# Column sums over the token blocks on GpSimd, and a new order of all steps, in an attention and feed-forward kernel

## The chip, the cores and the metric

The kernel runs on one core of one Trainium2 chip. The metric is the device time of one execution in microseconds (us); the median of the runs counts. The core has five engines with a queue of its own each: TensorE (PE, matrix products, with its weight loads shown as PEld), VectorE (DVE), ScalarE (ACT), GpSimd (POOL), and SyncE (SP), which issues DMAs. An engine works off its queue in order and waits on semaphores for what other engines make. Sums of products are built up in PSUM, which has eight banks.

## What is computed

There are B = 8 batches, H = 8 heads, S = 512 tokens, Ns = 32 state rows and D = 64 channels. Tokens attend to the state rows, state rows attend to the tokens, and both results pass through one feed-forward layer with 512 inputs, 2048 hidden units and 512 outputs.

```python
scores = scale * np.matmul(x, state.transpose(0, 1, 3, 2))
a = np.exp(scores - scores.max(-1, keepdims=True))
a /= a.sum(-1, keepdims=True) + 1e-09
xread = np.matmul(a, state)
scores2 = scale * np.matmul(state, x.transpose(0, 1, 3, 2))
a2 = np.exp(scores2 - scores2.max(-1, keepdims=True))
a2 /= a2.sum(-1, keepdims=True) + 1e-09
sread = np.matmul(a2, x)
attn = np.concatenate([xread, sread], axis=2)
# x: attn with the heads side by side, 8 * 544 rows of 512
h = x @ w_in
s = np.sin(alpha * h)
out = (h + s * s / (alpha + 1e-09)) @ w_out
```

The second softmax uses the same exponentials as the first, summed over the 512 tokens instead of over the 32 state rows: these are the column sums of the title.

## The kernel before, in words

The kernel has no loops over tiles in its code. A class has one short method for each step, and a long string, ORDER, names every step with its arguments in the order in which it is to be issued. Each engine gets its share of the steps in that order. Arguments name the batch or tile, the piece, the PSUM bank and, at the end, the engine (A is ACT, V is DVE, G is POOL). A tile is the 512 tokens of a batch (tiles 0 to 7) or all 256 state rows (tile 8). Heads are held in two groups g of four; a batch's tokens in four blocks i of 128.

For each batch:

- `lx` loads x with a DMA on POOL's queue; `pk` copies it in another arrangement (xp); `td` transposes it with a DMA on SP's queue (xT). For batches 0 and 1 PE transposes instead (`xtq`, `xt`, copies `xq` and `xc`).
- `sc` (PE) makes the scores; `ex` (ACT) the exponentials E, with tokens on the partitions; `rs` and `rr` (DVE) the sums over the state rows and their reciprocals; `nm` (POOL before) multiplies them in, giving A; `ad` (a DMA on SP) transposes A to AT. For batch 0, `at` and `ac` do so with PE and a copy.
- `m` (PE) multiplies the state with a quarter of w_in, M, in products that use a 64 by 32 part of PE's array each, eight side by side; `me` (ACT or DVE) copies M from PSUM to SBUF.
- `w` (PE) multiplies E, summed over the tokens, with x: the unnormalised result of the state rows, 16 products. `cs` (PE) multiplies each of the four token blocks of E with a column of ones, once for either row r of a pair of heads, into 64 of the 128 PSUM partitions: the column sums, 8 products of half width for a batch. `rc` (DVE) takes the reciprocal of them and `xs` (DVE) multiplies it in, into xs_all.

For each tile t and each of 16 blocks f of 128 hidden units:

- `h` (PE) makes the hidden values in two products (four for tile 8, which reads xs_all of all batches and w_in); for tile 0 the two are separate steps, `hg`.
- `si` (ACT) takes the sine, `sq` (ACT, DVE or POOL) squares it, `gt` (DVE) multiplies by 1/alpha and adds h, giving gT, the input of the second product. gT lies in a pool of 38 buffers.
- `o` (PE) adds up the output of 128 rows (st) over the 16 blocks f, in one PSUM bank; `oc` (ACT or DVE) copies it to one of six buffers and `os` stores it with a DMA on SP's queue. The last part of tile 7 is split into two pieces of columns (`oh`, `och`, `osh`).

A step may use a PSUM bank only after the bank's last value has been read. Two steps of one tile's output need not be neighbours: `o` has two arguments f0 and f1, and ORDER names the run f0 to f1 of blocks each time, always from 0 upward. `warm_up` steps issue products of zeros, whose results nobody reads.

Lines of the profile that the prediction uses: 201 products of elementwise type (squares, and A), 255 the cast of the first state rows, 282 the loads of w_in, 399 `sc`, 410 `rs`, 416 `rr`, 406 `ex`, 450 `w`, 461 `cs`, 468 `rc`, 471 `xs`, 488 `m`, 496 `me`, 537, 543 and 552 `h`, 560 `si`, 569 `sq` on ACT, 576 `gt`, 587 `o`, 595 `oc`, 602 and 605 `os` (605 for the state rows).

Of the kernel before, what the change touches and what calls it, by code (L numbers as in the profile page):

```python
# [21 lines left out]
touch_x l_s01 consts touch lq.0.S ident_ l_alpha lq.1.S zero.0 warm_up.7.512.3 exp_table lq.2.S  # L22
zero.1 identf.V lq.3.S s01_c.G l_st li.0 xq.0.A s01_t.4 li.1 xtq.0.5 warm_up.1.384.3 xq.1.A
s01_k.1.V s01_k.0.A li.2 xtq.1.6 warm_up.2.448.3 xc.0.0.0.V xq.2.A xc.0.0.1.V lo.0 al_t.7 xq.3.A
xtq.2.0 warm_up.1.384.3 al_c inva sc.0.0.1 lo.1 xc.0.1.0.A warm_up.1.256.3 xtq.3.2 warm_up.2.128.3
ex.0.0 warm_up.2.128.4 lx.1.0.1 warm_up.2.128.5 xc.0.1.1.V warm_up.2.128.6 warm_up.2.128.7 rs.0.0
sc.0.1.0 li.3 st_t.0.3 ex.0.1 rr.0.0 st_t.1.4 lo.2 st_c.0.0.V st_c.0.1.A warm_up.2.128.5
warm_up.2.128.6 warm_up.2.128.1 st_c.1.0.A rs.0.1 warm_up.2.128.2 warm_up.2.128.7 nm.0.0.0.4.G
warm_up.2.128.0 warm_up.2.128.5 st_c.1.1.A warm_up.2.128.3 warm_up.2.128.6 warm_up.2.128.1 rr.0.1
warm_up.2.128.2 sin_table warm_up.2.128.7 warm_up.2.128.0 nm.0.1.0.4.G at.0.0.5 warm_up.2.128.3  # L30
ac.0.0.V m.0.0.6.4 m.1.0.1.2 lo.3 at.0.1.7 me.0.0.0.V me.0.0.1.A warm_up.2.128.0 warm_up.2.128.3
me.1.0.1.A ac.0.1.V hg.0.2.0.5 me.1.0.0.V hg.0.1.0.4 hg.0.2.1 hg.0.1.1 hg.0.0.0.0 lx.2.0.1 si.0.2
hg.0.0.1 m.1.1.6.3 si.0.1 m.0.1.7.2 hg.0.3.0.1 me.0.1.1.A sq.0.2.V hg.0.3.1 sq.0.1.G me.1.1.0.V
me.1.1.1.A warm_up.2.128.2 gt.0.2 si.0.0 warm_up.2.128.2 warm_up.2.128.6 warm_up.2.128.3
warm_up.2.128.2 warm_up.2.128.6 me.0.1.0.A gt.0.1 sq.0.0.G m.0.2.3.2 si.0.3 m.1.2.5.6 hg.0.4.0.7
me.0.2.0.V me.0.2.1.A hg.0.4.1 sq.0.3.G hg.0.6.0.4 me.1.2.1.V hg.0.6.1 si.0.4 hg.0.7.0.3 hg.0.11.0.2
me.1.2.0.V si.0.6 hg.0.7.1 sq.0.4.G hg.0.5.0.6 gt.0.0 hg.0.5.1 si.0.7 hg.0.11.1 hg.0.8.0.5 hg.0.8.1
sq.0.6.A gt.0.3 sq.0.7.G o.0.3.0.2.0 si.0.5 gt.0.4 o.0.3.2.3 o.0.0.0.2.1 si.0.11 o.0.0.2.3 gt.0.6
sq.0.5.G o.0.0.3.4 o.0.2.0.1.7 si.0.8 o.0.3.3.5 sq.0.11.A gt.0.7 hg.0.9.0.4 sq.0.8.G o.0.2.1.2
gt.0.5 o.0.2.2.4 hg.0.9.1 gt.0.11 o.0.0.4.5 hg.0.10.0.3 si.0.9 o.0.2.4.5 gt.0.8 o.0.0.5.6 o.0.3.5.6  # L40
sq.0.9.A o.0.3.6.8 pk.1.0.V hg.0.10.1 xt.1.1.6 pk.1.1.V si.0.10 gt.0.9 xt.1.0.2 xc.1.1.0.A sq.0.10.G
o.0.2.5.6 xc.1.1.1.V xc.1.0.0.A o.0.0.6.7 xc.1.0.1.V o.0.0.7.8 o.0.2.6.7 sc.1.1.5 gt.0.10 sc.1.0.4
m.0.3.6.2 ex.1.0 o.0.2.7.8 me.0.3.0.V o.0.1.0.3.3 me.0.3.1.V o.0.1.3.6 hg.0.13.0.6 o.0.1.6.7 ex.1.1
rs.1.0 hg.0.13.1 m.1.3.2.4 si.0.13 o.0.1.7.8 rr.1.0 rs.1.1 nm.1.0.0.4.G o.0.1.8.9 hg.0.12.0.5
o.0.3.8.9 rr.1.1 hg.0.12.1 me.1.3.0.V o.0.0.8.9 nm.1.1.0.4.G o.0.1.9.10 o.0.0.9.10 me.1.3.1.V
si.0.12 o.0.0.10.11 o.0.3.9.11 sq.0.13.G ad.1 hg.0.15.0.2 sq.0.12.A o.0.1.10.12 hg.0.15.1 gt.0.12
o.0.2.8.10 si.0.15 o.0.2.10.11 gt.0.13 o.0.0.11.12 hg.0.14.0.4 sq.0.15.A hg.0.14.1 o.0.3.11.13
si.0.14 gt.0.15 o.0.0.12.13 o.0.1.12.13 o.0.3.13.14 sq.0.14.A pk.2.0.V o.0.1.13.14 pk.2.1.V h.1.2.5
gt.0.14 h.1.4.6 td.2 si.1.2 lx.3.0.1 h.1.0.2 si.1.4 o.0.0.13.15 sq.1.2.V h.1.1.4 si.1.0 gt.1.2
sq.1.4.G o.0.3.14.16 si.1.1 o.0.2.11.13 sq.1.0.A oc.0.3.V h.1.6.5 sq.1.1.G gt.1.4 o.0.2.13.14 os.0.3  # L50
h.1.3.0 si.1.6 gt.1.0 o.0.1.14.16 si.1.3 sq.1.6.G h.1.13.6 gt.1.1 oc.0.1.A o.0.2.14.15 o.0.0.15.16
si.1.13 h.1.15.2 sq.1.3.G lx.4.0.1 gt.1.6 os.0.1 o.0.2.15.16 oc.0.0.A h.1.5.4 sq.1.13.V oc.0.2.V
si.1.15 h.1.7.3 os.0.0 gt.1.3 o.1.1.0.1.5 si.1.5 os.0.2 h.1.8.1 sq.1.15.G gt.1.13 o.1.1.1.2 si.1.7
o.1.2.0.2.7 sq.1.5.A o.1.1.2.3 sq.1.7.G h.1.12.0 gt.1.15 si.1.8 h.1.9.6 gt.1.5 o.1.2.2.3 si.1.12
sq.1.8.G o.1.2.3.5 gt.1.7 si.1.9 o.1.1.3.4 h.1.10.2 sq.1.12.A pk.3.1.V h.1.11.4 sq.1.9.G gt.1.8
o.1.2.5.6 si.1.10 o.1.2.6.7 gt.1.12 h.1.14.3 si.1.11 sq.1.10.G o.1.2.7.8 gt.1.9 sc.2.1.1 si.1.14
o.1.1.4.7 sq.1.11.A pk.3.0.V sq.1.14.G o.1.1.7.8 gt.1.10 td.3 o.1.2.8.9 sc.2.0.0 o.1.1.8.9 gt.1.11
o.1.1.9.10 ex.2.0 o.1.3.0.2.6 gt.1.14 o.1.3.2.4 o.1.2.9.10 o.1.3.4.5 o.1.2.10.12 ex.2.1 o.1.2.12.13
rs.2.0 o.1.1.10.11 m.2.2.2.4.3.0 rr.2.0 rs.2.1 o.1.2.13.14 nm.2.0.0.4.G me.2.3.0.A o.1.2.14.15 w.0.1
rr.2.1 me.2.2.1.A me.2.3.1.V o.1.3.5.6 nm.2.1.0.4.G me.2.2.0.A o.1.3.6.7 o.1.2.15.16 cs.0 oc.1.2.A  # L60
m.2.0.3.4.0.2 ad.2 rc.0 o.1.3.7.8 me.2.1.1.A o.1.3.8.9 sc.3.0.7 xs.0.1 me.2.1.0.A o.1.1.11.12 os.1.2
me.2.0.0.V sc.3.1.2 me.2.0.1.A o.1.1.12.13 o.1.3.9.10 xs.0.0 pk.4.1.V pk.4.0.V td.4 o.1.3.10.11
ex.3.0 o.1.1.13.16 ex.3.1 rs.3.0 o.1.3.11.13 oc.1.1.A o.1.3.13.14 rr.3.0 h.2.0.0 rs.3.1 nm.3.0.0.4.G
os.1.1 o.1.3.14.16 si.2.0 rr.3.1 h.2.1.3 oc.1.3.V nm.3.1.0.4.G h.2.2.4 h.2.8.1 os.1.3 h.2.3.7 ad.3
si.2.2 o.1.0.0.3.2 si.2.8 sq.2.0.V o.1.0.3.4 sq.2.2.G gt.2.0 h.2.4.5 si.2.1 o.1.0.4.6 si.2.3
sq.2.8.G o.1.0.6.7 gt.2.2 h.2.9.6 si.2.4 o.2.3.0.1.0 o.1.0.7.8 sq.2.1.G o.1.0.8.9 sq.2.3.A gt.2.8
o.1.0.9.10 h.2.5.4 si.2.9 gt.2.3 o.1.0.10.11 sq.2.4.G o.1.0.11.12 si.2.5 h.2.7.1 gt.2.1 o.1.0.12.13
sq.2.9.A sq.2.5.G o.1.0.13.14 gt.2.4 o.1.0.14.15 si.2.7 o.1.0.15.16 o.2.0.0.1.7 gt.2.9 o.2.0.1.2
oc.1.0.A h.2.6.3 sq.2.7.G gt.2.5 o.2.3.1.2 os.1.0 o.2.3.2.3 si.2.6 h.2.10.5 o.2.3.3.4 sq.2.6.A
o.2.3.4.5 gt.2.7 h.2.11.6 si.2.10 h.2.12.2 gt.2.6 si.2.11 o.2.0.2.3 sq.2.10.G o.2.0.3.4 o.2.3.5.6  # L70
si.2.12 h.2.15.4 h.2.13.1 sq.2.11.A gt.2.10 sq.2.12.G o.2.0.4.5 si.2.15 h.2.14.3 gt.2.11 o.2.3.6.7
si.2.13 o.2.0.5.6 sq.2.15.G gt.2.12 o.2.0.6.8 si.2.14 o.2.3.7.9 sq.2.13.A o.2.3.9.10 gt.2.15
sq.2.14.G o.2.0.8.11 gt.2.13 o.2.0.11.12 sc.4.0.5 sc.4.1.6 gt.2.14 o.2.3.10.12 ex.4.0 o.2.3.12.13
w.1.2 cs.1 o.2.0.12.13 rc.1 o.2.3.13.15 ex.4.1 o.2.3.15.16 m.3.0.4.1.3.5 rs.4.0 oc.2.3.A o.2.0.13.14
me.3.1.0.A o.2.0.14.15 os.2.3 me.3.0.0.V o.2.1.0.1.6 me.3.0.1.A o.2.1.1.2 o.2.0.15.16 rr.4.0 rs.4.1
o.2.1.2.3 me.3.1.1.A nm.4.0.0.4.G h.3.1.0 oc.2.0.A o.2.1.3.4 rr.4.1 xs.1.0 m.3.2.3.4.1.5 si.3.1
nm.4.1.0.4.G os.2.0 xs.1.1 h.3.0.7 me.3.2.0.V h.3.2.2 ad.4 me.3.3.0.V o.2.1.4.6 lx.5.0.1 o.2.2.0.1.3
me.3.3.1.V si.3.2 o.2.2.1.3 si.3.0 h.3.6.1 sq.3.1.V sq.3.2.G me.3.2.1.V h.3.14.5 si.3.6 o.2.2.3.4
gt.3.1 o.2.2.4.5 sq.3.0.G si.3.14 o.2.2.5.7 gt.3.2 o.2.2.7.8 sq.3.6.A o.2.2.8.9 h.3.8.4 sq.3.14.G
gt.3.0 h.3.5.0 si.3.8 gt.3.6 h.3.15.2 si.3.5 o.2.2.9.10 sq.3.8.G gt.3.14 o.2.2.10.11 h.3.9.7 si.3.15  # L80
h.3.7.1 si.3.9 sq.3.5.G gt.3.8 o.2.2.11.13 si.3.7 h.3.10.5 sq.3.9.G o.2.2.13.14 sq.3.15.A gt.3.5
# [76 lines left out]
class Steps:  # L158
# [449 lines left out]
    def oh(k, t, st, half, bank):  # L608
        k.o(t, st, 0, k.FT, bank, half=half)
# [54 lines left out]
```

## Time and profile before

| | |
|---|---|
| median of 3 runs | 221.41 us (221.36 to 221.83) |
| the profiled execution | 221.22 us |
| its span, from first to last event | 219.2 us |
| TensorE busy | 211.4 us |
| column sums on PE (line 461) | 64 products |
| warm-up products (line 303) | 66 |

The profile is of one execution. A page of it gives for each engine the time in which it was busy, a chain of work followed back from the last instruction, and groups of instructions with their number, busy time, mean length, and the idle time before them with what ended it. A timeline lists instructions by start time. A matmul's length includes the time in which its result runs out of the array while the next one is already under way, so the distance from start to start tells what one costs in a stream; a few records of matmuls are missing.

### The profile page before, as it was taken

How to read it: one execution, taken by the hardware profiler on the slowest of the kernel's cores; microseconds unless marked ns; L12 is line 12 of the kernel's file. 1: busy time of each engine (PE TensorE's matmuls, PEld its weight loads, DVE VectorE, ACT ScalarE, POOL GpSimd, SP SyncE). 2: the span in 40 equal slices, each digit the busy share in tenths (PEclk: the TensorE clock that was granted, in tenths of full speed). 3: DMA queues.
4: the chain of work that ended last, by engine and by line, in shares of the span. 5: the costliest groups of instructions: out<-in, count | busy, mean ns of one | idle time of the engine just before them, and what ended most of it. 6: DMA issues, size and time to landing. Idle time of an engine off the chain costs nothing.

```text
span 219.2 us, 4303 instructions
## 1 busy us (share of the span) xinstructions
PE 211.4 (96%) x1593; PEld 104.5 (48%) x1619; DVE 162.9 (74%) x287; ACT 173.4 (79%) x297; POOL 106.2 (48%) x114
## 2 busy tenths in 40 slices
PE   7989999999999999999999999999999999999994
PEld 3744544444444534444454444454445555665452
DVE  3769996999787789989888788888667987661201
ACT  4799778997998979898996999798848896785111
POOL 5959533895195647753943387273501082121000
PEclk9999999999999999999999999999999999999999
DMA  6999999987491029167145327470220211012042
GB/s 195 178 206 204 205 204 146 217 169 133 101 238 48 3 92 143 57 144 96 48 79 131 109 71 96 134 110 0 48 100 0 98 48 48 0 51 96 1 143 96
DMA packets 38052, 23.48 MB, mean 107 GB/s; under 512 B 20992, under 2 KB 33680, under 8 KB 38032
## 3 DMA queue, kind: packets, MB, share of 16 engines
q1 hardware_dynamic: 26128, 15.08, 26.5%
q0 software_dynamic: 11648, 8.13, 26.0%
q8 instruction: 12, 0.20, 0.3%
q14 instruction: 8, 0.07, 0.1%
q10 hardware_dynamic: 256, 0.01, 0.1%
HBM read 17.44 MB, written 8.91 MB: 120 GB/s over the span
## 4 chain that ended last, share of the span: by engine, by line
PE 90%; DMA 6%; POOL 1%; issue 1%; ACT 0%
PE o_ps L587 54%; PE h_ps L537 22%; DMA w_in_sb<-in_moe_w_in_dram 5%; PE m_ps L488 4%; PE h_ps L543 3%; PE h_ps L552 2%; PE w_ps L450 2%; PE s_ps L399 2%; PE w_ps L461 1%; DMA s<-in_state_dram 1%; POOL w_in_sb L282 1%; PE x_ps L376 0%; POOL st_nat L267 0%; POOL s01b L255 0%; ACT o_sb L595 0%
## 5 line engine op out<-in xcount | busy, mean ns | idle before, releaser
L587 PE MATMUL o_ps<-w_out_sb,gT 128*128 128x512 bf16 (+2 forms) x542 | 133.9, 373 | 1.6 <-issue 1.0
L576 DVE SCALAR_TENSOR_TENSOR gT<-s,inva_sb,h_ps 128x512 bf16<-128x512 bf16 (+1 forms) x144 | 96.8, 713 | 20.4 <-POOL s L201 10.8
L201 POOL TENSOR_TENSOR s<-s 128x512 bf16<-128x512 bf16 (+1 forms) x75 | 75.9, 1022 | 64.4 <-ACT s L560 62.7
L560 ACT ACTIVATE s<-h_ps,alpha_sb 128x512 bf16<-128x512 f32 (+1 forms) x144 | 88.8, 670 | 11.1 <-PE h_ps L543 4.5
L587 PEld LDWEIGHTS <-gT 128*128 128x128 bf16 x560 | 52.3, 98 | 60.3 <-issue 5.0
L537 PE MATMUL h_ps<-AT,M 128*128 128x512 bf16 x219 | 60.0, 379 | 0.3
L537 PEld LDWEIGHTS <-M 128*128 128x128 bf16 x224 | 21.7, 98 | 25.9 <-issue 0.4
L569 ACT ACTIVATE s<-s 128x512 bf16<-128x512 bf16 (+1 forms) x53 | 31.4, 594 | 0.8
L201 POOL TENSOR_TENSOR A<-E,rR 128x512 bf16<-128x512 bf16 x16 | 16.6, 1056 | 23.8 <-ACT o_sb L595 12.9
L595 ACT COPY o_sb<-o_ps 128x512 f32<-128x512 f32 (+2 forms) x24 | 13.7, 570 | 16.6 <-PE o_ps L587 16.5
L496 ACT CAST M<-m_ps 128x512 bf16<-128x512 f32 x35 | 18.6, 594 | 8.2 <-PE m_ps L488 8.2
L496 DVE CAST M<-m_ps 128x512 bf16<-128x512 f32 x29 | 18.9, 679 | 2.5 <-PE m_ps L488 2.1
L595 DVE COPY o_sb<-o_ps 128x512 f32<-128x512 f32 x11 | 7.5, 685 | 12.9 <-PE o_ps L587 12.9
L201 DVE TENSOR_TENSOR s<-s 128x512 bf16<-128x512 bf16 (+1 forms) x16 | 7.0, 439 | 6.2 <-ACT s L560 6.1
L410 DVE TENSOR_REDUCE R<-E 128x16 f32<-128x512 bf16 x16 | 10.4, 657 | 0.7 <-ACT E L406 0.6
L488 PE MATMUL m_ps<-w_in_sb,stT 64*32 64x512 bf16 x256 | 10.2, 382 | 0.1
L468 DVE RECIPROCAL rC<-w_ps 128x128 f32<-128x128 f32 x8 | 7.6, 948 | 3.3 <-PE w_ps L461 3.2
L303 PE MATMUL warm_ps<-warm 128*128 128x128 bf16 (+3 forms) x66 | 8.6, 271 | 1.4 <-DVE warm L209 1.2
L552 PE MATMUL h_ps<-AT,M 128*128 128x512 bf16 x29 | 8.4, 379 | 0.9 <-ACT M L496 0.7
L406 ACT ACTIVATE E<-s_ps 128x512 bf16<-128x512 f32 x16 | 8.8, 602 | 0.4 <-PE s_ps L399 0.4
L543 PE MATMUL h_ps<-xs_all,w_in_sb 128*128 128x256 bf16 x64 | 9.1, 273 | 0.0
L543 PEld LDWEIGHTS <-w_in_sb 128*128 128x128 bf16 x64 | 6.3, 98 | 3.4
(56 smaller groups left out, 101.8 us busy)
## 6 DMA issues: line engine op xcount, KB each, us to landing
out_dram<-o_sb SPq DMA_DIRECT2D x33, 256.0 KB, 2.3
xnat<-in_x_dram POOLq DMA_DIRECT2D x7, 512.0 KB, 7.5
w_in_sb<-in_moe_w_in_dram POOLq DMA_DIRECT2D x4, 512.0 KB, 10.9
w_out_sb<-in_moe_w_out_dram POOLq DMA_DIRECT2D x4, 512.0 KB, 18.0
x<-in_x_dram SPq DMA_DIRECT2D x4, 256.0 KB, 4.2
st_nat<-in_state_dram POOLq DMA_DIRECT2D x1, 256.0 KB, 5.3
out_dram<-o_sb SPq DMA_DIRECT2D x1, 192.0 KB, 1.9
s<-in_state_dram SPq DMA_DIRECT2D x1, 128.0 KB, 2.2
```

Of the source, the lines that this page charges most:

```text
L201: {"V": k.nc.vector, "G": k.nc.gpsimd}[eng].tensor_tensor(out, a, b, ALU.mult)
L410: k.nc.vector.reduce_sum(R[:, g], k.t["E", b][:, g].rearrange("p c (h j) -> p (c h) j", j=k.Ns), axis=AX.X)
L488: k.nc.tensor.matmul(k.t["m", b, s + n, g][o0:o0 + k.Ns, :], k.stT[k.half(r), b * k.G + g, c0:c0 + k.Ns], k.w_in_sb[k.half(r), 2 * g + h, ...
L496: k.copy(eng)(k.t["M", b][:, g, s * k.FW:(s + 1) * k.FW], k.t["m", b, s, g][:])
L537: k.nc.tensor.matmul(hp[:, :n], k.t["M", t][:, g, fs], k.t["AT", t][:, g, :], start=(g == 0), stop=(g == k.G - 1),)
L543: k.nc.tensor.matmul(hp[:, :n], k.w_in_sb[:, q, fs], k.xs_all[:, q].rearrange("p b j -> p (b j)"), start=(q == 0), stop=(q == k.Q - 1),)
L552: k.nc.tensor.matmul(k.t["h", t, f][:], k.t["M", t][:, g, f * k.P:(f + 1) * k.P], k.t["AT", t][:, g, :], start=(g == 0), stop=(g == k.G - 1),)
L560: k.nc.scalar.activation(s[:, :n], k.t["h", t, f][:, :n], ACT.Sin, scale=k.alpha_sb[:, f:f + 1])
L569: k.nc.scalar.activation(s2[:, :n], s[:, :n], ACT.Square)
L576: k.nc.vector.scalar_tensor_tensor(gT[:, :n], k.t["s2", t, f][:, :n], k.inva_sb[:, f:f + 1], k.t["h", t, f][:, :n], ALU.mult, ALU.add,)
L587: k.nc.tensor.matmul(k.t["o", t, st, half][:, cols], k.t["gT", t, f][:, rows], k.w_out_sb[:, f, cols], start=(f == 0), stop=(f == k.FT - 1),)
L595: k.copy(eng)(o_sb[:, cols], k.t["o", t, st, half][:, cols])
```

## The change

The column sums are made in two stages. For each batch POOL adds up the four token blocks of E: `ca` adds blocks 0 and 1 to blocks 2 and 3 in fp32, `cb` adds the two results. `ch` copies the sum as bf16 (the high part) and `cl` subtracts that copy from the sum and writes the rest as bf16 (the low part). The sum over the partitions stays on PE, now in the step `w`, behind its 16 products: four products for a batch, for either row r and for the high and low part, with a stationary operand `sel` of 128 columns, of which 64 are ones and 64 zeros, so that all 128 partitions of PSUM are written each time. `cs` is gone.

```diff
-        k.ones = const.tile([P, k.D], BF16, name="ones")
+        k.sel = const.tile([P, 3 * k.D], BF16, name="sel")
...
+        k.sump, k.hlp = pool("sump", 1), pool("hlp", 2)
...
-        k.nc.vector.memset(k.ones[:], 1.0)
+        k.nc.vector.memset(k.sel[:].bitcast(U32), 0)
+        k.nc.vector.memset(k.sel[:, k.D:2 * k.D], 1.0)
...
+    def ca(k, b):
+        k.t["sum", b] = k.sump.tile([k.P, 2, k.G, k.P], FP32, name="sum")
+        E = k.t["E", b][:].rearrange("p g i c -> p i g c")
+        k.nc.gpsimd.tensor_tensor(k.t["sum", b][:], E[:, 0:2], E[:, 2:4], ALU.add)
+
+    def cb(k, b):
+        t = k.t["sum", b]
+        k.nc.gpsimd.tensor_tensor(t[:, 0], t[:, 0], t[:, 1], ALU.add)
+
+    def ch(k, b):
+        hl = k.new(b, "hilo", k.hlp, [k.P, 2, k.G, k.P], BF16)
+        k.nc.gpsimd.tensor_copy(hl[:, 0], k.t["sum", b][:, 0])
+
+    def cl(k, b):
+        hl = k.t["hilo", b]
+        k.nc.gpsimd.tensor_tensor(hl[:, 1], k.t["sum", b][:, 0], hl[:, 0], ALU.subtract)
...
     def w(k, b, bank):
...
-
-    def cs(k, b):
-        E, wc = k.t["E", b], k.t["w", b]
-        for i in range(k.C):
-            for r in range(2):
-                Ev = E[:, :, i, :].rearrange("p g (h r j) -> p g h r j", h=2, r=2)
+        for r in range(2):
+            for p in range(2):
+                Ev = k.t["hilo", b][:, p].rearrange("p g (h r j) -> p g h r j", h=2, r=2)
                 k.nc.tensor.matmul(
-                    wc[k.half(r), :, 2 * k.Ns:], k.ones[:], Ev[:, :, :, r],
-                    start=(i == 0), stop=(i == k.C - 1),
+                    wc[:, :, 2 * k.Ns:], k.sel[:, (1 - r) * k.D:(3 - r) * k.D], Ev[:, :, :, r],
+                    start=(r == 0 and p == 0), stop=(r == 1 and p == 1),
                 )
...
-    def o(k, t, st, f0, f1, *bank, half=None):
+    def oo(k, t, st, bank, half=None):
+        k.t["o", t, st, half] = k.ps(bank, [k.P, k.DOUT], FP32, "o_ps")
+        k.made["o", t, st, half] = 0
+
+    def o(k, t, st, f, half=None):
         cols = k.cols(half)
...
+        k.made["o", t, st, half] += 1
+        k.nc.tensor.matmul(
+            k.t["o", t, st, half][:, cols], k.t["gT", t, f][:, rows], k.w_out_sb[:, f, cols],
+            start=k.made["o", t, st, half] == 1, stop=k.made["o", t, st, half] == k.FT,
+        )
```

The steps `o` and `hg` no longer have to follow the order of f and of g: `oo` and `ho` take the bank, and a counter tells which product is the first and which the last of a sum.

ORDER is new from the first step to the last. What is on which engine changes with it:

| steps | before | after |
|---|---|---|
| `sq`, tiles 0 to 7: ACT, DVE, POOL | 42, 15, 71 | 35, 42, 51 |
| `sq`, tile 8: ACT, DVE, POOL | 11, 1, 4 | 3, 7, 6 |
| `nm`: DVE, POOL | 0, 16 | 4, 12 |
| `me`: ACT, DVE | 35, 29 | 37, 27 |
| `oc` and `och`: ACT, DVE | 24, 11 | 24, 11 |
| `xq`: ACT, DVE | 4, 0 | 2, 2 |
| warm-up products | 66 | 17 |
| `ca`, `cb`, `ch`, `cl` on POOL | 0 | 8 each |

The numbers of `h`, `o`, `m`, `sc`, `si` and `gt` are the same. The loads on POOL's queue stand in the same order at the start. On SP's queue the stores of a tile come later than before, often behind the transposes of the next batches: the first store stands behind `td` of batch 3, the last four are those of tile 7's rows 0, tile 8's two parts and the last piece of tile 7.

## The prediction

> **What bounds the kernel now.** I read the page first: busy shares, granted clock, chain that ended last. Then the chain's first 25 us, TensorE's waits and TensorE's timeline round the column sums, then the groups by shape, for prices.
>
> ```profile
> span 219.2 us, 4303 instructions
> PE 211.4 (96%) x1593; PEld 104.5 (48%) x1619; DVE 162.9 (74%) x287; ACT 173.4 (79%) x297; POOL 106.2 (48%) x114
> PEclk9999999999999999999999999999999999999999
> PE 90%; DMA 6%; POOL 1%; issue 1%; ACT 0%
> ```
>
> TensorE (PE) is busy for 96% of the span, at the full granted clock in every slice, and it is 90% of the chain. The other 10% are mainly the start and the last store:
>
> ```profile
> 5.58 11.79 DMA w_in_sb<-in_moe_w_in_dram
> 17.41 0.62 PE m_ps L488 x16
> ...
> 20.73 2.16 PE o_ps L587 x10
> ```
>
> Up to 17.4 us PE goes from one landing piece of w_in to the next, filling with warm-up products. From 17.4 us to its last product at 216.1 us the chain stays on PE. The waits of PE after 20.5 us are one line (us in total, times, longest):
>
> ```profile
> PE o_ps L587 <- issue: 1.0, 6, 0.2
> ```
>
> So the time is the landing of w_in's third piece, plus PE's list of products, plus the store. A gain must shorten that list. A loss is any moment in which PE stands.
>
> ```profile
> 54.74 0.81 PE L587 MATMUL o_ps<-w_out_sb,gT 128*128 128x512 bf16 x3
> 55.48 0.41 PE L461 MATMUL w_ps<-E,ones 128*64 128x128 bf16 x8
> 55.83 0.63 PE L488 MATMUL m_ps<-w_in_sb,stT 64*32 64x512 bf16 x16
> 76.11 0.63 PE L450 MATMUL w_ps<-E,xp 128*128 128x64 bf16 x16
> 76.67 0.41 PE L461 MATMUL w_ps<-E,ones 128*64 128x128 bf16 x8
> 77.02 1.04 PE L587 MATMUL o_ps<-w_out_sb,gT 128*128 128x512 bf16 x4
> 215.12 1.00 PE L587 MATMUL o_ps<-w_out_sb,gT 128*128 128x128 bf16 x15
> ```
>
> Columns are start, length, engine, line. A group's length has the last product's run-out in it, so the price on PE is start to next start: 0.345 us for the 8 column-sum products (76.67 to 77.02, 55.48 to 55.83). They use half of the array's columns, two at a time, and going over to the split array costs more: 3 outputs of 0.216 us after 54.74 end at 55.39, the sums start 0.094 later. The last line gives a product with 128 columns on the whole array, each with its own weight load: (1.00 - 0.22) / 14 = 0.056 us.
>
> **The change, part by part.** *Removed from PE*: 64 half-width sums. The timeline has six runs of 8 at 0.345 and one of 16 (batches 7 and 5) at 0.570: 2.64 us. All seven runs pay the 0.094; four are followed at once by M products, which then pay none themselves, so 3 x 0.094 = 0.28 goes for good. Together 2.92 us.
>
> *Added on PE*: 32 full-width sums, four behind each w, no change of the array's split: 32 x 0.056 = 1.79 us. Net -1.13 us, all on the path, since PE never waits there.
>
> The Trainium skill's page TensorE: Matmul & The Clock Gate (Back-to-back issue gap) gives about 81 ns for each product in a stream of loads and products of 128 columns. By it the 32 would be estimated at 2.6 us and the net gain at 0.3. The row at 215.12 is the same form on this chip, and I take the row.
>
> *M products regrouped* (8 each): after the first outputs there were 2 runs of 8 and 12 of 16, there will be 2 of 8, 9 of 16 and 2 of 24. A run of 16 takes 0.558 start to start, 8 more add 0.216: 12 x 0.558 = 6.70 against 9 x 0.558 + 2 x 0.774 = 6.57. One entry less, 0.09. Together -0.22.
>
> *Head*: POOL's queue issues the loads in the same order, so w_in's pieces land as before (first products into M at 11.9, 14.9, 17.4). When the first output product is issued PE has in both versions done the same 20 h products and 6 groups of 8 into M, at 20.57 us before. Walking the new order with the rows: the second M run's copies (0.6 us each) allow five h products before 17.1, the third M run goes at 17.4, its neighbour waits for gT of tile 0 until about 18.6, eight h products follow, first output at 20.3. I take -0.1; -0.3 to +0.6 are the ends, the upper if a POOL square (1.05) stands before each such copy.
>
> *Tail*: before, PE ended at 216.12 and the span at 219.2. The last small store now stands behind a state-row store on SP (line 605: 0.78 and 0.61 us to issue; line 602: 0.34). It can start some 0.25 us later: +0.25.
>
> *Other engines*, off the path while the next products are ready:
>
> ```profile
> L576 DVE SCALAR_TENSOR_TENSOR gT<-s,inva_sb,h_ps 128x512 bf16<-128x512 bf16 x128 | 89.5, 742 | 12.4 <-POOL s L201 8.5 <-ACT s L569 2.7
> L201 POOL TENSOR_TENSOR s<-s 128x512 bf16<-128x512 bf16 x71 | 73.4, 1045 | 54.3 <-ACT s L560 52.6
> L569 ACT ACTIVATE s<-s 128x512 bf16<-128x512 bf16 x42 | 26.9, 640 | 0.5
> L201 POOL TENSOR_TENSOR A<-E,rR 128x512 bf16<-128x512 bf16 x16 | 16.6, 1056 | 23.8 <-ACT o_sb L595 12.9 <-DVE rR L416 5.9 <-issue 3.0
> L201 DVE TENSOR_TENSOR s<-s 128x512 bf16<-128x512 bf16 x15 | 6.7, 449 | 6.2 <-ACT s L560 6.1
> L255 POOL CAST s01b<-s 128x256 bf16<-128x256 f32 x1 | 0.4, 396 | 1.7 <-DMA s<-in_state_dram 1.7
> ```
>
> POOL: no row has an fp32 sum. The first add (512 elements) is nearest to 1.056, a product of the same size with an fp32 operand; the second and the subtraction have half, 0.612 by the 256-wide squares; the copy is the 0.396 cast. 2.68 us for a batch, 21.4 in all; bounds 8 x 1.6 (every step at the cast's price) and twice the row, 43. Against it 20 wide squares less (-20.9), 2 narrow more (+1.2), 4 normalisations less (-4.2): 106.2 becomes about 104, at most 125, of 219.
>
> The Trainium skill's GPSIMD Engine Reference (Engine selection) speaks against this part: elementwise work belongs on VectorE, GpSimd takes about twice as long for two inputs. Its 4497 ns for 2048 fp32 elements scale to an estimate of 1.1 us for 512, like the row. It would move the sums to DVE, which has less room.
>
> DVE: 27 wide squares more (12.1), 6 narrow (6 x 0.285 = 1.7), 4 normalisations (no row; between the square's 0.449 and gT's 0.742, I take 0.742 for the fp32 operand: 3.0), 2 x-casts for 2 M-copies less (0). 162.9 becomes 180, 83% of the new span. ACT loses 7 wide and 8 narrow squares and two x-casts, and gets two M-copies: 173 becomes 166.
>
> *New wait*: w now waits for the subtraction. Behind it on PE stands everything; xs, then the state rows' h, wait for it. Counting PE products between, the subtraction is ordered far ahead for batches 0, 1, 2 and 3, and right before w for 5 and 7. There POOL is nearly free. Batch 7 is tightest: its copy reuses the buffer that w of batch 6 reads, and 4.3 us of PE work lie from that w to the next, for 0.40 + 0.61 us of POOL work. Cost 0; at the double price still 0.
>
> *Smaller margins*: from h to the first output that uses its gT, PE has 10.4 us of other work in the median before and 7.8 after; over what the chain sin, square, gT needs, 8.3 and 5.6. The smallest margin goes from 0.73 to 0.54. I allow 0.3 us for stops of PE (0 to 0.8).
>
> Sum: -1.13 - 0.22 - 0.1 + 0.25 + 0.3 = -0.9. The profiled execution took 221.22 (2.0 outside its span), the median of the runs is 221.41; from the median 220.5, and without the stops 220.2. The latter is my forecast, as half of the gTs have over 5 us to spare. Its own range is 219.3 to 220.9: the ends of the head and of the stops, and nothing for the store.
>
> **Rivals.** *VectorE becomes the bound.*
>
> ```profile
> 50.00:100.00 50.00, 49.52 (x372) 22.66 (x385) 42.53 (x74) 44.73 (x75) 30.49 (x30) 1.00 0.48 102
> ```
>
> PE, loads, DVE, ACT, POOL in the stretch from 50 to 100 us: DVE is busy for 42.5 of 50. The new order has over the same PE work 6 squares, 2 normalisations and 5 gTs more and 1 copy less: +7.5, so 50 of 50. The 5 gTs (3.7) may come later, so 46.3 has to be done. DVE stood for 7.5 us here before, mostly for squares of other engines. If half of that stays, 50.0 us are needed and nothing is lost: this is the point from which it decides. At three quarters it costs 1.9, at all of it 3.8; I take the middle, 2.8: 223.0, slower. For it: 10 us at 40 to 50 show DVE 9.96 busy already. Against: PE lost nothing there.
>
> *The change of PE's list is real but given back* (full-width sums at 0.08, more stops, a slower head): -0.5 at best, 220.97 to 221.85: no change.
>
> *The sums come late*, PE stands at w: for batch 7 that starts where copy and subtraction take over 4.3 us, 4.3 times the rows; at six times it is 6.1 - 4.3 = 1.8 us: 222.0. Against it stands POOL's 52% of idle time.
>
> **How the numbers follow.** Forecast 0.56, given back 0.13, VectorE 0.26, sums late 0.05. A measurement can tell 0.2% (0.44 us) from no change. Forecast gives faster 0.57 with a sliver of the ties; same 0.14; slower 0.29 from VectorE and the late sums. The range runs from 219.0 (the forecast's lower end with the head's and no later store) to 223.0 (VectorE's price).
>
> **What would show it.** Right: 7 column-sum runs gone, 32 products at 0.056 behind w, no entry before them, PE's last product near 214.7, PE's waits still about 1 us. Wrong: PE or weight loads waiting for gT at 50 to 100 us, or for POOL's hilo at w; a third M run later than 17.4; POOL's fp32 add well over 1.1 us.

## The result, and the profile after

The changed kernel takes 231.94 us in the median of 6 runs (230.82 to 233.76), the kernel before 221.56 beside it (221.12 to 221.83): 1.047 times as long, 95% interval 1.043 to 1.052. The forecast was 220.2, with a range from 219.0 to 223.0: it had the wrong sign, and the time lies far above the range. Where one run of a kernel was over 1.5% above the fastest of the same kernel (262.4 and 230.16 us below), the ratio leaves it out.

The head of the page of the changed kernel:

```profile
span 230.5 us, 4129 instructions
PE 213.2 (92%) x1510; PEld 102.0 (44%) x1538; DVE 184.9 (80%) x324; ACT 170.3 (74%) x283; POOL 108.2 (47%) x124
PEclk9999999999999998899999999999999999999997
PE 61%; DVE 25%; ACT 5%; DMA 2%; issue 2%; POOL 1%; SPq 1%; ACTq 0%; POOLq 0%
```

The chain that ended last was 90% PE and had nothing of VectorE (DVE) in it; now a quarter of it is DVE. Two slices on the way have a clock below full (the last slice too, when PE is done). TensorE's (PE's) timeline tells where the 11.3 us of span went (start, length, engine and line). This is the first group of output products before, then the first and the last of the changed kernel:

```profile
20.57 2.32 PE L587 MATMUL o_ps<-w_out_sb,gT 128*128 128x512 bf16 x10
```

```profile
19.90 1.89 PE L612 MATMUL o_ps<-w_out_sb,gT 128*128 128x512 bf16 x8
...
210.74 12.07 PE L612 MATMUL o_ps<-w_out_sb,gT 128*128 128x512 bf16 x70
```

Before, the first output product started at 20.57 and the last ended at 216.12, with 3.1 us to the span's end. Now it is 19.90, 222.82 (210.74 + 12.07, unrounded) and 7.7. From first to last output product there were 195.55 us; the forecast took 1.35 us of products out of this stretch (1.13 for the sums, 0.22 for M), so 194.2 should have stayed. It takes 202.92.

| part of the span | forecast | measured |
|---|---|---|
| to the first output product | -0.1 | -0.67 |
| products taken out of PE's list | -1.35 | (inside the next row) |
| from first to last output product, against 194.2 | +0 to +0.8 | +8.7 |
| from PE's end to the span's end | +0.25 | +4.6 |

-0.67 - 1.35 + 8.7 + 4.6 = 11.3. So two places are to be explained: PE loses 8.7 us on the way, and the end is 4.6 us longer. The waits of PE and of its weight loads (PEld) name the engine (us in total, times, longest):

```profile
PE h_ps L557 <- DVE gT L599: 2.7, 2, 2.3
...
PE s_ps L405 <- DVE gT L599: 0.7, 1, 0.7
PE s_ps L405 <- ACT xT L391: 0.7, 1, 0.7
```

```profile
PEld L612 <- DVE gT L599: 3.2, 9, 0.6
```

The products wait for PSUM banks that gT has not yet read, the weight loads for gT itself (0.2 us in all before the change). 0.7 us go to a copy of x on ScalarE (ACT). PE never waits for the sums made on GpSimd (POOL). The groups by shape show what DVE did meanwhile; the first line is of the kernel before, the others are of the changed kernel:

```profile
L348 DVE COPY xp<-xnat 128x1024 bf16<-128x1024 bf16 x14 | 5.5, 429 | 0.1
```

```profile
L599 DVE SCALAR_TENSOR_TENSOR gT<-s,inva_sb,h_ps 128x512 bf16<-128x512 bf16 x128 | 90.4, 743 | 7.2 <-ACT s L592 4.3 <-POOL s L206 1.0
L206 POOL TENSOR_TENSOR s<-s 128x512 bf16<-128x512 bf16 x51 | 54.1, 1065 | 53.8 <-ACT s L583 50.6 <-DVE s L206 0.8 <-DVE gT L599 0.8
L206 DVE TENSOR_TENSOR s<-s 128x512 bf16<-128x512 bf16 x42 | 22.3, 534 | 6.4 <-ACT s L583 6.2
L354 DVE COPY xp<-xnat 128x1024 bf16<-128x1024 bf16 x14 | 8.2, 606 | 0.0
L206 DVE TENSOR_TENSOR A<-E,rR 128x512 bf16<-128x512 bf16 x4 | 5.9, 1473 | 0.1
L454 POOL TENSOR_TENSOR sum<-E 128x512 f32<-128x512 bf16 x8 | 9.5, 1182 | 0.2
```

DVE's wide squares became longer, 534 ns in place of 449; its x-copies 606 in place of 429; a normalisation (A) takes 1473, twice the upper bound of the forecast. gT alone is what it was: 743. In the trace the long ones are those that run beside an instruction of POOL. Of the 42 squares, 25 have at most half of their time beside an instruction of POOL and take 361 to 426 ns; the 17 with more than half take 418 to 1140, 743 in the median. The costliest place, from the timeline:

```profile
84.91 1.05 POOL L206 TENSOR_TENSOR A<-E,rR 128x512 bf16<-128x512 bf16 x1 [4.13 <-ACT s L583]
86.03 3.44 DVE L206 TENSOR_TENSOR A<-E,rR 128x512 bf16<-128x512 bf16 x1
86.86 2.04 POOL L206 TENSOR_TENSOR s<-s 128x512 bf16<-128x512 bf16 x2
89.84 2.72 DVE L599 SCALAR_TENSOR_TENSOR gT<-s,inva_sb,h_ps 128x512 bf16<-128x512 bf16 x4
90.64 1.52 PE L557 MATMUL h_ps<-AT,M 128*128 128x512 bf16 x4 [2.30 <-DVE gT L599]
```

One normalisation on DVE lasts 3.44 us, through both squares of POOL (which end at 88.90) and 0.57 us more. Behind it in DVE's queue stand the gTs that free the banks, and PE stands for 2.30 us. Then the granted clock halves for 3.4 us. These are windows of 1 us with the busy time of PE, loads, DVE, ACT and POOL, then the clock:

```profile
91.00:92.00 1.00, 1.00 (x5) 0.34 (x3) 1.00 (x3) 0.60 (x1) 0.00 (x0) 0.51 1.27 233
92.00:93.00 1.00, 1.00 (x4) 0.25 (x2) 0.64 (x2) 0.78 (x2) 0.83 (x1) 0.50 1.13 356
```

This costs about 1.7 us of the 8.7 in the profiled execution. Four of the other five have a mean clock of 0.994 or 0.995 over the whole span: 0.6% of 232 us is 1.4 us, which leaves no room for such a stretch. They took 230.82 to 233.76 us all the same.

### The profile page after: what moved, and what is told of

It is laid out like the page before. It is cut to its first block, busy times and chain, and to the rows that moved or that the text cites. A ratio compares the mean times of both kernels' runs of the same rounds, so it can differ in the third digit from the quotient of the medians.

```text
span 230.5 us, 4129 instructions
## 1 busy us (share of the span) xinstructions
PE 213.2 (92%) x1510; PEld 102.0 (44%) x1538; DVE 184.9 (80%) x324; ACT 170.3 (74%) x283; POOL 108.2 (47%) x124
## 4 chain that ended last, share of the span: by engine, by line
PE 61%; DVE 25%; ACT 5%; DMA 2%; issue 2%; POOL 1%; SPq 1%; ACTq 0%; POOLq 0%
PE o_ps L612 37%; PE h_ps L557 14%; DVE gT L599 13%; DVE s L206 4%; PE m_ps L508 3%; PE h_ps L563 3%; ACT s L583 2%; DMA x<-in_x_dram 2%; DVE M L516 2%; DVE A L206 1%; DVE xp L354 1%; PE w_ps L473 1%; PE s_ps L405 1%; ACT M L516 1%; DVE R L416 1%
## 5 line engine op out<-in xcount | busy, mean ns | idle before, releaser
L612 PE MATMUL o_ps<-w_out_sb,gT 128*128 128x512 bf16 (+2 forms) x540 | 137.8, 374 | 1.8 <-issue 0.5
L206 POOL TENSOR_TENSOR s<-s 128x512 bf16<-128x512 bf16 (+1 forms) x57 | 57.8, 1017 | 69.3 <-ACT s L583 56.8
L557 PE MATMUL h_ps<-AT,M 128*128 128x512 bf16 x220 | 62.5, 381 | 3.0 <-DVE gT L599 2.7
L206 DVE TENSOR_TENSOR s<-s 128x512 bf16<-128x512 bf16 (+1 forms) x49 | 24.3, 498 | 7.6 <-ACT s L583 7.4
L206 POOL TENSOR_TENSOR A<-E,rR 128x512 bf16<-128x512 bf16 x12 | 12.7, 1064 | 29.0 <-DVE rR L422 12.7
L592 ACT ACTIVATE s<-s 128x512 bf16<-128x512 bf16 (+1 forms) x38 | 23.2, 614 | 0.9
L620 ACT COPY o_sb<-o_ps 128x512 f32<-128x512 f32 (+1 forms) x24 | 13.6, 575 | 13.3 <-PE o_ps L612 13.2
L620 DVE COPY o_sb<-o_ps 128x512 f32<-128x512 f32 (+1 forms) x11 | 7.4, 676 | 8.3 <-PE o_ps L612 8.3
L454 POOL TENSOR_TENSOR sum<-E 128x512 f32<-128x512 bf16 x8 | 9.5, 1182 | 0.2
L575 PE MATMUL h_ps<-AT,M 128*128 128x512 bf16 x29 | 8.5, 381 | 0.2 <-ACT M L516 0.2
L354 DVE COPY xp<-xnat 128x1024 bf16<-128x1024 bf16 x14 | 8.2, 606 | 0.0
```

What stands on the lines that cost most here:

```text
L206: {"V": k.nc.vector, "G": k.nc.gpsimd}[eng].tensor_tensor(out, a, b, ALU.mult)
L354: k.copy(eng)(k.t["xp", b][:, :, hs, :], k.t["xnat", b][:, hs, :].rearrange("p h (i d) -> p i h d", i=k.C),)
L557: k.nc.tensor.matmul(hp[:, :n], k.t["M", t][:, g, fs], k.t["AT", t][:, g, :], start=(g == 0), stop=(g == k.G - 1),)
L592: k.nc.scalar.activation(s2[:, :n], s[:, :n], ACT.Square)
L612: k.nc.tensor.matmul(k.t["o", t, st, half][:, cols], k.t["gT", t, f][:, rows], k.w_out_sb[:, f, cols], start=k.made["o", t, st, half] == 1 ...
L620: k.copy(eng)(o_sb[:, cols], k.t["o", t, st, half][:, cols])
```

## The experiments

Each run is set against the kernel before on the same chip. "On the way" is the time from the first to the last output product over 194.2 us, as in the table above: 8.7 for the changed kernel. Some expectations count the stops from the start of the products on, by the weight loads against the list of products; by that count it is 8.9 to 9.4.

### Is it the sums or the order?

The order of before, with the sums on POOL: `ca`, `cb`, `ch` and `cl` of each batch are put together into a stretch in which POOL was idle, and the 4 products (`ws`) stand where `cs` stood.

```diff
 (ORDER of before)
+ca.0 cb.0 ch.0 cl.0 nm.1.0.0.4.G
...
-cs.0
+ws.0
```

> The order of before; its 64 half-width column sums are replaced by the sums on POOL, put into POOL's idle stretches, and 32 full-width products at the same places on PE. If the column sums themselves cost the time (theory S), this kernel is slower than before by several us, with PE waiting at w_ps or POOL late. If the loss comes from the new order alone (theory O), it is about 1.1 us faster than before (64 sums at 2.92 us for 32 at 1.79 us): near 220.3 us.

Measured: 220.06 us (219.8 to 221.67, 10 runs), 0.994 of before, interval 0.992 to 0.997. It is faster than both kernels. PE's first and last groups of output products there:

```profile
20.53 2.32 PE L608 MATMUL o_ps<-w_out_sb,gT 128*128 128x512 bf16 x10
...
204.78 10.13 PE L608 MATMUL o_ps<-w_out_sb,gT 128*128 128x512 bf16 x62
```

The last product ends at 214.91, so the stretch is 194.38 us, 1.17 shorter than before; the forecast's sum for the sums alone was 1.13. The price of 0.056 us for a product, taken from the row, holds: four of them take 0.22 us from start to next start in the changed kernel (78.62 to 78.84). The estimate from the 81 ns of the Trainium skill's page TensorE: Matmul & The Clock Gate (Back-to-back issue gap) was a gain of 0.3, which does not agree.

The opposite: the new order with the column sums of before (`cs` behind `w`, nothing of them on POOL).

```diff
 (ORDER of after)
-ca.0 cb.0 ... ch.0 ... cl.0
...
-w.0.7
+w.0.7 cs.0
```

> The new order, but with the 64 half-width sums behind w and no sums on POOL. Theory S: close to before, 222 to 224 us. Theory O (the order loses the time, the sums do not): close to the changed kernel, 230 to 233 us. In between if POOL's 25 us of sums are what holds up the VectorE instructions that need two inputs from SBUF (theory P with the sums as its cause): 226 to 229 us.

Measured: 233.14 us (232.28 to 233.9), 1.052 times before, interval 1.047 to 1.057; on the way 9.9 us, of which 1.1 are its longer list. The largest stop is where it was:

```profile
PE h_ps L558 <- DVE gT L600: 2.5, 2, 2.1
```

So the order with its choice of engines costs the time, and not the sums on POOL, which by the medians gain in it too (233.14 - 231.94 = 1.2, though the intervals overlap).

### What holds DVE up: sharing with POOL, or too much work?

First a single step: the second normalisation of batch 4 goes back to POOL.

```diff
-nm.4.1.0.4.V
+nm.4.1.0.4.G
```

> The changed kernel with one normalisation of batch 4 moved from VectorE back to POOL: it took 3.44 us on VectorE beside POOL's work, and PE stood for 2.3 us behind it, then ran at a lower clock. Theory P (the instruction stood because POOL was at work): PE's 2.3 us stop at 88 to 91 us goes and with it the lower clock: 3 to 4 us faster, about 228 us. Theory D (VectorE is overloaded in this stretch by the number of its instructions): 0.7 us less work, at most 1 us faster.

Measured: 231.04 us (230.43 to 231.56), ratio 1.042, interval 1.036 to 1.044. The stop of 2.3 us is gone, but another one follows some steps later:

```profile
91.01 2.06 DVE L599 SCALAR_TENSOR_TENSOR gT<-s,inva_sb,h_ps 128x512 bf16<-128x512 bf16 x3 [2.12 <-POOL s L206]
93.13 0.63 PE L508 MATMUL m_ps<-w_in_sb,stT 64*32 64x512 bf16 x16 [1.39 <-DVE gT L599]
```

POOL now has the normalisation and its squares come later; DVE waits 2.12 us for one, and PE 1.39 for DVE. On the way 6.4 us are left (the 1.7 us of the halved clock there are gone too), but the first output product of this profile is 1.7 us later (the clock was halved from 8.5 to 11.9 us). The time alone, 0.9 us less, lies where the expectation put theory D; that the stop went speaks for theory P. A single step moved does not settle it.

Next, both engines are measured by themselves. The kernel below leaves the whole computation out, and repeats forms of DVE on tiles of the same shapes.

```python
for v, nv in ((v_square, 16), (v_xcopy, 16), (v_norm, 12), (v_gt, 12), (v_mcopy, 12)):
    for g in (None, g_square, g_add) if v is v_square else (None, g_square):
        meet()                      # each engine waits for the other
        for _ in range(nv): v()     # VectorE
        for _ in range(12 if g else 0): g()   # GpSimd
```

> The kernel computes nothing of the reference (it writes zeros). It repeats five operations of VectorE on tiles of the kernel's shapes, each first with GpSimd idle and then beside a run of 512-wide squares on GpSimd, and the square also beside 512-wide fp32 sums on GpSimd. Theory sharing (VectorE and GpSimd hinder each other in certain instructions): square 0.42 us alone and 0.6 to 1.1 beside GpSimd, x-copy 0.42 alone and about 1 beside, normalisation about 0.68 alone and over 0.87 beside, gT (one operand in PSUM) 0.74 in both, copy out of PSUM the same in both. Rival, too much work for VectorE and nothing else: every pair equal within 5%, and the long squares in the changed kernel come from something else, such as waits counted as work.

The instructions were issued in another order than written, squares and copies of DVE in turn, and the copy out of PSUM met no work of POOL; the pairs can be read all the same. From its timeline:

```profile
14.39 1.29 POOL L76 TENSOR_TENSOR g_out<-g_in 128x512 bf16<-128x512 bf16 x1
14.70 1.25 DVE L56 TENSOR_TENSOR v_out<-v_in 128x512 bf16<-128x512 bf16 x1
15.64 1.22 POOL L79 TENSOR_TENSOR g_sum<-g_in 128x512 f32<-128x512 bf16 x1
15.88 1.26 DVE L67 COPY x_out<-x_in 128x1024 bf16<-128x1024 bf16 x1
16.81 1.22 POOL L76 TENSOR_TENSOR g_out<-g_in 128x512 bf16<-128x512 bf16 x1
```

One instruction of DVE is done for each of POOL, 1.18 us apart: 1.26 us (median) for a square or an x-copy, against 0.41 alone. POOL's own go from 1.04 to 1.22. gT takes 0.748 in both cases. The rival's "equal within 5%" is refuted.

The second kernel of this kind (computing nothing of the reference either) keeps the order as written and takes more forms of both engines.

```python
for g in (None, g_square, g_copy, g_scale, g_set):
    for v in (v_square, v_norm, v_xcopy, v_scale, v_stt, v_hsquare, v_gt, v_mcopy, v_sum):
        meet()
        for _ in range(10 if g else 0): g()   # GpSimd
        for _ in range(8): v()                # VectorE
```

> The kernel computes nothing of the reference. Nine forms of VectorE, eight instructions of each, first with GpSimd idle and then beside ten instructions of GpSimd: two-input square, one-input copy, one-input scale, fill. Theory one at a time (either engine takes the pair of read paths of SBUF for a whole instruction): forms of VectorE with two operands in SBUF and copies in the fast mode (square, normalisation, x-copy, scale, two-operand scalar form) wait for the GpSimd instruction that runs, 0.41 becomes 1.2 us beside squares, and forms with an operand in PSUM (gT, square against PSUM, copy out of PSUM) and the row sum stay within 2%. If GpSimd's one-input forms hinder as much as its square, the hindrance lies with the engine; if not, with its two-input form. Rival, bandwidth shared evenly: times grow by a common factor below 2 in all SBUF forms, whatever GpSimd does.

Squares (L57) and gTs (L65) of DVE alone, and then beside POOL's squares (L77), eight each, from its timeline:

```profile
4.09 3.63 DVE L57 TENSOR_TENSOR v_out<-v_in 128x512 bf16<-128x512 bf16 x8
...
31.92 6.23 DVE L65 SCALAR_TENSOR_TENSOR v_out<-v_in,one,h 128x512 bf16<-128x512 bf16 x8
...
49.65 7.95 DVE L57 TENSOR_TENSOR v_out<-v_in 128x512 bf16<-128x512 bf16 x8
50.15 12.75 POOL L77 TENSOR_TENSOR g_out<-g_in 128x512 bf16<-128x512 bf16 x10
...
112.96 11.09 POOL L77 TENSOR_TENSOR g_out<-g_in 128x512 bf16<-128x512 bf16 x10
113.94 6.21 DVE L65 SCALAR_TENSOR_TENSOR v_out<-v_in,one,h 128x512 bf16<-128x512 bf16 x8
```

Eight squares go from 3.63 to 7.95 us, eight gTs stay at 6.2. Medians of one instruction, in ns:

| DVE, 512 wide | POOL idle | beside POOL's square | beside POOL's copy | beside POOL's fill |
|---|---|---|---|---|
| square, both operands in SBUF | 424 | 1144 | 712 | none met |
| normalisation | 693 | 1410 | 979 | 692 |
| x-copy (1024 wide) | 427 | 1145 | 712 | 495 |
| scale by a constant | 294 | 1081 | 635 | 360 |
| gT (one operand in PSUM) | 748 | 748 | 748 | 748 |
| square against PSUM | 687 | 686 | 687 | 686 |
| copy out of PSUM | 691 | 691 | 692 | 691 |
| sums along a row | 686 | 686 | 686 | 686 |

Two classes stand apart. The first four are held up by an amount that depends on POOL's instruction and hardly on DVE's: beside POOL's square (1.04 alone) 0.72 to 0.79 us are added, beside its copy (0.61) 0.29 to 0.34, so it is not a common factor. With the one-for-one order of the run before, this reads as turns of whole instructions. The last four notice nothing. POOL's copy has one input and hinders too, so it is not its two-input form alone; its scale by a constant, which the table leaves out, added 0.29 us to two of eight squares and three of eight normalisations. The Trainium skill's GPSIMD Engine Reference (Specifications) says that GpSimd shares its SBUF interfaces with VectorE, with contention for VectorE instructions in a two-port mode or with two SBUF inputs. Our rows agree: square, normalisation and the fast one-input forms are hit, gT is not. That POOL's fill hardly hinders (692 ns for the normalisation, 495 for the x-copy) makes it useful: it can stand in for POOL's time with little of the sharing.

The three runs that follow use this in the changed kernel. In the first, every square and normalisation is back on the engine that it had before, in the new order.

```diff
-sq.0.3.V sq.0.0.V sq.0.1.G sq.0.2.G sq.0.4.G sq.0.5.A ...
+sq.0.3.G sq.0.0.G sq.0.1.G sq.0.2.V sq.0.4.G sq.0.5.G ...
```

> The changed kernel with its own order of steps, but every square and every normalisation on the engine that it had before (105 of the steps change engine). VectorE gets 27 wide squares and 4 normalisations less, GpSimd 20 and 4 more. Theory VectorE (its load and its sharing with GpSimd make the stops up to 100 us): the 8.9 us that PE loses on the way fall to 2 to 3, the tail's 4.5 stays: 224 to 227 us. Rival, the order of PE's list leaves too little time between h and output whatever the engines do: 230 or more.

Measured: 260.06 us (258.26 to 262.4), ratio 1.171, interval 1.163 to 1.178. The theory's 224 to 227 was far off; the time lies in the rival's range, 230 or more. The waits tell why:

```profile
POOL s L206 <- ACT s L583: 73.1, 39, 7.7
DVE gT L599 <- POOL s L206: 44.5, 40, 3.3
```

DVE is busy for only 64% of this span, but stands 44.5 us before gTs whose squares POOL has not done. In the order of before, nine steps (median) stand between a square on POOL and its gT, and never none; in this run it is one, and none for 35 of the 71 (full tiles). So the run does not speak on sharing. It shows that the choice of engines belongs to its order, and that a lightly loaded DVE does not help when what heads its queue waits.

In the second, POOL's squares of full tiles are left out, and gT takes the sine itself.

```diff
-        if eng == "A":
+        if eng == "G" and t < k.B:
+            k.t["s2", t, f] = s
+        elif eng == "A":
```

> The changed kernel with the squares of full tiles on GpSimd left out (gT of these takes the sine itself); VectorE has the same instructions. Theory sharing: VectorE's wide squares fall back to 0.42 each and its x-copies to 0.42, so its busy time falls by 7 to 11 us, the stops up to 100 us go to under 2 us, and the time is 223 to 226 us (the tail stays). Rival, VectorE has too many instructions even at their undisturbed prices: busy time falls too, but PE still loses 5 us or more and the time is 228 or more. What this does not tell apart: gT no longer waits for a square that GpSimd has late.

Measured: 226.4 us (225.27 to 230.16), ratio 1.020, interval 1.012 to 1.028. From first to last output product 196.22 us, 2.0 on the way in place of 8.7. DVE's squares take 449 ns and its x-copies 462, where 0.42 us was expected for both. The time lies just above the 223 to 226 of the theory, and below the rival's 228. But gT has lost a possible wait as well.

The third keeps that wait and POOL's time. In place of a square POOL copies two elements of the sine, then fills (the squares' values are left out).

```diff
+        if eng == "G" and t < k.B:
+            k.nc.gpsimd.tensor_copy(s2[:, 0:2], s[:, 0:2])
+            for c in (k.S, k.S, k.S // 2):
+                k.nc.gpsimd.memset(s2[:, 0:c].bitcast(U32), 0)
-        if eng == "A":
+        elif eng == "A":
```

> The changed kernel in which GpSimd's squares of full tiles are left out, but not its time: in place of each stands a copy of two elements of the sine (so that it waits for it as before, and gT waits for GpSimd as before) and three fills, 0.24 + 0.31 + 0.31 + about 0.2 = 1.06 us, forms that did not hold up VectorE's two-input forms when measured alone. VectorE's instructions are the same. Theory sharing: VectorE's wide squares fall from 534 to under 470 ns, its x-copies from 606 to under 510, its normalisations to about 1000; PE loses 3 to 5 us on the way in place of 9.4, and the time is 225 to 228 us, near the 226.4 of the run without these squares. Rival, gT waits for GpSimd and VectorE has too many instructions: 230 or more, as in the changed kernel.

Measured: 226.45 us (226.32 to 227.59), ratio 1.024, interval 1.021 to 1.027. Page and groups by shape of this run:

```profile
PE 210.0 (94%) x1510; PEld 101.8 (45%) x1538; DVE 178.0 (79%) x324; ACT 169.7 (76%) x283; POOL 106.0 (47%) x277
...
L594 POOL MEMSET s<- 128x256 uint32 x102 | 31.7, 311 | 5.9
L206 DVE TENSOR_TENSOR s<-s 128x512 bf16<-128x512 bf16 x42 | 18.2, 436 | 6.2 <-ACT s L583 5.8
L354 DVE COPY xp<-xnat 128x1024 bf16<-128x1024 bf16 x14 | 7.2, 529 | 0.4 <-DMA xnat<-in_x_dram 0.4
L206 DVE TENSOR_TENSOR A<-E,rR 128x512 bf16<-128x512 bf16 x4 | 3.3, 814 | 0.1
```

POOL is as busy as in the changed kernel (106.0 and 108.2 us), DVE has the same 324 instructions, and each square is waited for. The sharing with these squares is gone: DVE's squares fall to 436 ns (expected under 470), normalisations to 814; the x-copies, at 529, miss the expected 510 by a little, as POOL's sums and normalisations still run beside some. On the way 2.3 us are left of 8.7. So 6.4 us of the loss is DVE held up by POOL's squares, and what it sets off, the halved clock of that profile (1.7) included; by the medians the fills gain 5.5 us. DVE's greater number of instructions can, without this sharing, have no more than the other 2.3, and 0.7 of these is again the wait for ACT's copy:

```profile
PE s_ps L405 <- ACT xT L391: 0.7, 1, 0.7
```

The sharing in turn costs nothing where DVE has room. In the run with the order of before and the sums on POOL, POOL is busier still (131.1 us) and DVE's x-copies take 496 ns, but DVE is busy for only 42.9 us of the 50 from 50 to 100, and PE stands for none of them. It takes both.

### What makes the end longer?

The changed kernel ends with two stores of the state rows and one small piece of tile 7. One theory was the queue of six late stores on SP. Its last 39 products `o` are grouped by output, in the order 7.1, 7.2, 7.0, first piece of 7.3, 8.1, 8.0, last piece of 7.3, so that the stores spread out. Two late stores of tiles 5 and 6 go a little ahead as well.

```diff
 h.8.14.3 ...
-o.8.0.3 o.8.1.2 o.7.1.14 o.8.1.10 ... oc.7.1.A os.7.1 ... oc.8.0.V oh.7.3.1.6
+o.7.1.14 ... os.7.1 o.7.2.2 ... os.7.2 o.7.0.5 ... os.7.0 oh.7.3.0.1 ... o.8.1.2 ... os.8.1 ...
```

> The changed kernel with the last 39 output products grouped by output, so that the six last stores start 1 to 3 us apart and not within 4 us. If the 7.6 us from PE's last product to the end of the span (3.1 before) are six stores queued on the DMA engines, the time falls by 3.5 to 4.5 us, to about 228 us. If they are SP's issue or something else, it falls by less than 1 us.

Measured: 230.35 us (230.24 to 230.9), ratio 1.040, interval 1.036 to 1.044. The gain is 1.6, less than half of what was expected. From PE's last product to the span's end it takes 5.7 us in place of 7.7, and PE has a new stop of 0.57 us, made by the edit:

```profile
212.20 11.22 PE L612 MATMUL o_ps<-w_out_sb,gT 128*128 128x512 bf16 x67 [0.57 <-DVE gT L599]
```

So the queue was not the whole. Now the two outputs of the state rows come before the last two of tile 7, as in the kernel before. The copies of 8.0 and 7.0 swap engines with it.

```diff
-... os.7.2 o.7.0.5 ... os.7.0 oh.7.3.0.1 ... o.8.1.2 ... os.8.1 o.8.0.3 ... oh.7.3.1.6 ... os.8.0 osh.7.3.1
+... os.7.2 o.8.1.2 ... os.8.1 o.8.0.3 ... os.8.0 o.7.0.5 ... os.7.0 oh.7.3.0.1 ... oh.7.3.1.6 ... osh.7.3.1
```

> The changed kernel with the last 39 output products grouped by output in the order 7.1, 7.2, 8.1, 8.0, 7.0, 7.3: the two outputs of the state rows are stored before the last two of tile 7, as in the kernel before. Theory slow state-row stores (their transfers take 4 to 6 us, the others 2): from PE's end to the span's end 7.6 us become 3 to 4, and the time is 227.5 to 229 us, unless PE stands anew for gT of tile 8. Rival, the queue of SP: no better than the 230.35 of the run that stored them last but spread out.

Measured: 228.49 us (227.64 to 229.86), ratio 1.031, interval 1.025 to 1.038. From PE's end to the span's end 2.9 us, a little under what was expected; the stop of 0.57 us at tile 8 is there too. The store of the last 64 KB piece, from issue to landing (the last figure, us), in the kernel before, the changed one, the one with the spread end and this one:

```profile
out_dram<-o_sb SPq DMA_DIRECT2D x1, 64.0 KB, 1.8
```

```profile
out_dram<-o_sb SPq DMA_DIRECT2D x1, 64.0 KB, 5.9
```

```profile
out_dram<-o_sb SPq DMA_DIRECT2D x1, 64.0 KB, 4.2
```

```profile
out_dram<-o_sb SPq DMA_DIRECT2D x1, 64.0 KB, 1.6
```

The same 64 KB take 1.6 to 1.8 us behind stores of tile 7, and 4.2 to 5.9 right behind one of the state rows. In the kernel before the store behind them was slow too (issued 209.82, landed 214.22), but PE went on until 216.12 and hid it. Why a store of the state rows takes so long, and holds up what follows, was not tried.

Last, both edits together, fills and the order of the end.

> Both edits together, fills for GpSimd's squares and the state rows' outputs before the last two of tile 7. If sharing and the store of the state rows are the two causes and independent, 3.0 to 4.5 us less than with the fills alone: 221.5 to 224.5 us. If the end of the run is set by something else that the two runs moved together, less than 2 us of gain.

Measured: 223.13 us (222.09 to 223.6), ratio 1.008, interval 1.005 to 1.010; 3.3 less than with the fills alone. The end is 2.9 us, 3.2 us are lost on the way (the new stop of tile 8 among them). The two gains add up (3.32 here, 3.45 for the order of the end alone), and together they take away 8.8 of the 10.4 us by which the changed kernel is slower. This run leaves squares out, so it is no version to use; the one that beats both kernels is the order of before with the sums on POOL.

## Why the prediction was wrong, point by point

- *The sums on PE, net -1.13*: right, in the size and in the row that it was taken from. -1.17 measured alone.
- *POOL's sums and the new wait at w*: right. A sum costs 1.18 + 0.78 + 0.44 + 0.67 = 3.07 us a batch in place of 2.68; PE never waits for it.
- *Head, -0.1*: the first output product came 0.67 us earlier, beyond the end of -0.3. It says little: in the two runs that change only the end of the order it came at 19.81 and 20.62.
- *M regrouped, -0.22*: not tried alone.
- *"DVE: 27 wide squares more (12.1) ... 4 normalisations (3.0) ... 180"*: this is the first step that failed, the price of DVE's work. Its prices were those of a DVE that met POOL seldom: in the profile of before two of its 15 wide squares lay beside an instruction of POOL and took 578 and 658 ns, the others 414 to 426, and the mean of 449 hid both. In the new order 17 of 42 lie beside one. The squares cost 22.3 us in place of 18.9 at 449 each, the x-copies 8.2 in place of 5.5, the normalisations 5.9 in place of 3.0. A price depends on what the neighbour does at the time.
- *"I allow 0.3 us for stops of PE (0 to 0.8)"*: measured 8.7, the largest miss of the sum. The margins from h to the output product were counted at undisturbed prices, and the stops were not set by the median margin. gT, which frees PSUM, stands behind everything else in DVE's queue, so one long instruction there makes PE stand. The fills take 6.4 of the 8.7 away. DVE's busy share does not tell it: from 50 to 100 us DVE was busy for 46.7 of 50 with 75 instructions, and with the fills for 46.6 with 83, while PE's busy time went from 46.2 to 49.0.
- *The rival "VectorE becomes the bound", 223.0*: right in its place and its engine, at a chance of 0.26, and too small. Its condition was how much of DVE's idle time stays; what decided was that DVE's own work grew by sharing, which no case had. The squares that DVE waits for, which it named, are not the cause: before the wide gTs DVE waits for POOL's for 1.0 us in all, where it was 8.5 before the change.
- *Tail, +0.25*: measured 4.6. The step counted the issue of the state rows' store on SP (0.78 and 0.61 us), not the time that its transfer holds up the one behind it. The last store was issued 0.88 us after PE's end (0.32 before), 0.56 later where 0.25 was counted, and then took 5.9 us to land in place of 1.8. The trace of before had it: the store behind the state rows' took 4.4 us to land where others took about 2, hidden under PE's last products.
- *The forecast's own range, 219.3 to 220.9*: it does not follow from the terms. Without a later store, and with the ends given for the head and the stops, they add up to 219.8 to 221.5 us.

Open are three things. About 2.3 us on the way remain after the fills, 0.7 of them the wait for ACT's copy; POOL's sums and normalisations still share there, DVE is still busy for 79%, and neither was tried alone. The 3.44 us of one normalisation are more than 0.69 and two squares of POOL give (2.73 in all). It also ran beside POOL's issue of a load; beside such issues alone the same normalisation took 1.21 us in the run without POOL's squares, but 0.69 in the one with fills. And the halved clock came after a stop of 2.3 us here; in the run with the engines of before a stop of 2.62 us was followed by full clock and one of 2.65 by 3.4 us at half, so what sets it is not settled.

## What to carry to other kernels

Before moving work to DVE or POOL, look at a group's lengths one by one, not at its mean: if some are two or three times the others, see what the neighbour did then, and price the move at the long value for the share that will meet it. Of the forms measured here, those with an operand in PSUM and the row sums were safe beside POOL; two-input and fast one-input forms in SBUF were not, beside POOL's square and copy. A long instruction does harm where the queue behind it has no room and holds what another engine waits for. At the end of a kernel, read the landing of the stores, not only their issue, and do not let a slow one be the last.

## What was not expected of the hardware

- DVE's forms in SBUF and POOL's squares ran one for one, in turn: a DVE scale of 0.29 us became 1.08 beside POOL's 1.04 us squares, and a normalisation 1.41. It goes both ways: POOL's square took 1.37 us beside DVE's normalisations.
- POOL's scale by a constant takes 1.49 us for 512 elements, longer than its two-input square (1.04) and its copy (0.61); its fill takes 0.31 and leaves DVE's normalisation at 0.69.
- A 64 KB store behind a store of the state rows lands after 4.2 to 5.9 us, elsewhere after 1.6 to 1.8.
